# Padding the rows of the v-and-gate weights from 642 to 648 columns

## Chip, cores and metric

The kernel runs on one core of one Trainium2 chip. The metric is the device time of one execution in microseconds (us). Ratios are given with a 95% interval.

## The reference

Two branches over 2048 tokens of width 640 are mixed by a gate per token: linear attention (32 heads of 20, Hedgehog feature maps) and a SwiGLU feed-forward of width 1728.

```python
x = A_x
g = sigmoid((x * gate_w).sum(-1, keepdims=True))
a = A_ref(x, A_wqkv, A_w_phi, A_wo)      # linear attention
# inside A_ref:  kv = einsum("bhsf,bhsd->bhfd", phi_k, v);  z = phi_k summed over s
b = B_ref(x, B_w_gate, B_w_up, B_w_down) # (silu(x wg) * (x wu)) wd
return g * a + (1 - g) * b
```

## The kernel before

Tokens are cut in 16 tiles of 128. The width 640 is cut in 5 chunks of 128, which are the contraction steps. Three pieces are shown: the tile `wvg`, whose rows hold the 640 v columns of a chunk, the gate column and one spare; the ten products of a v tile, two halves of 320 and 321 columns per chunk; and the eleven products of a kv tile, whose moving operands are 63 columns each in a v buffer.

```python
wvg = sb("wvg", [P, 5, D + 2], BF16)            # P = 128, D = 640
...
v1r = sb("v1r", [P, NV, 33 * 21], BF16)         # v tiles: 33 heads of 20 values and a one
...
def v_pairs(t, pr):
    # (output, stationary, moving, start, stop, ...)
    return [(bank(2 * pr + hb, 0, 320 + hb), xT[:, t, c, :],
             wvg[:, c, 320 * hb:640 + hb - 320 * (1 - hb)],
             c == 0, c == 4, False) for c in range(5) for hb in range(2)]
...
def kvtile(t):
    b = t % 4
    pairs = []
    for j in range(NCH):                        # NCH = 11
        bk, jj = (KV0, j) if j < 8 else (KV0 + 1, j - 8)
        o = bank(bk, 63 * jj, 63 * jj + 63)
        pairs.append((o, ekr[:, b, 120 * j:120 * j + P], vbuf(t)[:, 63 * j:63 * j + 63],
                      t == 0 and jj == 0, t == NT - 1, True))
    mm(pairs)
```

The order of all work on all engines is a fixed list in the kernel. `mm` issues one matmul per entry on one line, which is why nearly all of TensorE's work carries the line L296.

The softmax here doesn't subtract the row's maximum and nothing guards it: scores larger than these inputs give would overflow.

Of the kernel before, what the change touches and what calls it, by code (L numbers as in the profile page):

```python
# [6 lines left out]
P = 128  # L7
S_TOK = 2048
D = 640
# [17 lines left out]
BF16 = DT.bfloat16  # L27
# [169 lines left out]
def _build(nc, A_x, A_wqkv, A_w_phi, A_wo, B_x, B_w_gate, B_w_up, B_w_down, gate_w, out):  # L197
# [5 lines left out]
    def sb(name, shape, dtype):  # L203
        t = nc.alloc_sbuf_tensor(name, list(shape), dtype)
        tr.reg(t, "sbuf", nc.lookup_mloc(t).addr)
        return t

    xT = sb("xT", [P, NT, 5, P], BF16)
    wqk = sb("wqk", [P, 2, 5, D], BF16)
    wvg = sb("wvg", [P, 5, D + 2], BF16)  # L210
    wog = sb("wog", [P, 5, D], BF16)
    wd = sb("wd", [P, 14, D], BF16)
    wg = sb("wg", [P, 5, F_FFN], BF16)
# [555 lines left out]
def bass_gated_mix__linear_kernel_hedgehog__swiglu_ffn__prompt_kernel(  # L769
    nc: bass.Bass,  # L770
    A_x: bass.AP,
    A_wqkv: bass.AP,
    A_w_phi: bass.AP,
    A_wo: bass.AP,
    B_x: bass.AP,
    B_w_gate: bass.AP,
    B_w_up: bass.AP,
    B_w_down: bass.AP,
    gate_w: bass.AP,
    out: bass.AP,  # L780
):
    _build(nc, A_x, A_wqkv, A_w_phi, A_wo, B_x, B_w_gate, B_w_up, B_w_down, gate_w, out)
# [28 lines left out]
```

## Time and profile before

| | before |
|---|---|
| median of the first 3 runs | 288.74 us (288.39 to 288.85) |
| span of the profiled run | 287.0 us |
| TensorE (PE) busy | 99% of the span |
| next engine (VectorE) | 57% |
| v products | 160 of 1979 matmuls |

How to read it: what a matmul costs is the distance from its start to the next one's start, called the *interval* below. In the timeline of PE the columns are start, duration of the piece, engine, line, operation, output and inputs, stationary and moving shape, and the count. A tile's cost is the start of the following piece minus its own start. Where a finer table is given, it was read start by start from the same trace, as means over the 16 token tiles; intervals of more than 160 ns are left out of the tables by chunk.

### The profile page before, as it was taken

The page shows a single profiled execution, that of the slowest core. Times are in us where ns is not written, and L with a number is a line of the kernel's source. Part 1 is how long each engine was busy: PE and PEld are TensorE (multiplying, and loading weights), DVE is VectorE, ACT ScalarE, POOL GpSimd, SP SyncE. Part 2 cuts the span into 40 slices and gives each one's busy share as a digit, 9 for nine tenths or more (in the row PEclk, how much of TensorE's full clock was granted, in tenths as well). Part 3 has the DMA queues.
Part 4 walks back from the last instruction along what each step waited for, and adds up shares of the span by engine and source line. Part 5 has one row for each costly group of instructions (what it writes and reads, how often), then busy time and mean ns, then how long its engine had stood idle before and what let it go on. Part 6 is the DMA issues. An engine that isn't in the chain of part 4 may idle for free.

```text
span 287.0 us, 4972 instructions
## 1 busy us (share of the span) xinstructions
PE 284.1 (99%) x1979; PEld 174.5 (61%) x1979; DVE 163.3 (57%) x243; ACT 152.4 (53%) x256; POOL 159.8 (56%) x125
## 2 busy tenths in 40 slices
PE   8999999999999999999999999999999999999997
PEld 6667777575644545557775556675554446666776
DVE  2337748576569978689991465970317899100000
ACT  0767778576775465683535753225676552234112
POOL 8286999879446789836543438350754558501000
PEclk9999999999999999999999999999999999999999
DMA  7977697000010598202383002061020006210101
GB/s 234 192 113 127 113 279 279 3 1 2 0 50 0 123 290 162 50 2 50 66 157 69 6 1 50 2 149 43 2 50 0 3 1 123 53 46 0 49 23 48
DMA packets 48944, 21.62 MB, mean 75 GB/s; under 512 B 39384, under 2 KB 48792, under 8 KB 48920
## 3 DMA queue, kind: packets, MB, share of 16 engines
q1 hardware_dynamic: 47400, 20.43, 31.5%
q10 hardware_dynamic: 1520, 0.87, 1.0%
q8 instruction: 16, 0.26, 0.4%
q14 instruction: 8, 0.07, 0.1%
HBM read 9.29 MB, written 2.62 MB: 42 GB/s over the span
## 4 chain that ended last, share of the span: by engine, by line
PE 99%; DVE 0%; issue 0%
PE ps L296 97%; PE ps L478 1%; PE ps L308 0%; DVE xT L320 0%; DVE osb L737 0%; DVE wvg L320 0%
## 5 line engine op out<-in xcount | busy, mean ns | idle before, releaser
L324 POOL TENSOR_TENSOR hT<-hT,us 128x512 bf16<-128x512 bf16 (+1 forms) x56 | 65.0, 1174 | 65.1 <-DVE hT L328 47.5
L328 DVE SCALAR_TENSOR_TENSOR hT<-hT,ps 128x512 bf16<-128x512 bf16 (+1 forms) x56 | 37.4, 683 | 66.8 <-ACT hT L314 53.0
L296 PE MATMUL ps<-xT,wg 128*128 128x512 bf16 x260 | 64.6, 379 | 0.0
L296 PE MATMUL ps<-xT,wu 128*128 128x512 bf16 x260 | 64.6, 379 | 0.0
L296 PE MATMUL ps<-wd,hT 128*128 128x320 bf16 (+2 forms) x462 | 63.9, 295 | 0.0
L324 POOL TENSOR_TENSOR ph<-eq,qc 128x1320 bf16<-128x1320 bf16 x16 | 42.4, 2647 | 25.6 <-DVE qc L638 20.8
L296 PEld LDWEIGHTS ps<-wd,hT 128*128 128x128 bf16 x462 | 44.5, 98 | 17.5 <-issue 0.2
L296 PE MATMUL ps<-wqk,xT 128*128 128x320 bf16 x320 | 47.7, 299 | 0.0
L314 ACT ACTIVATE hT<-ps 128x512 bf16<-128x512 f32 (+2 forms) x64 | 36.4, 569 | 16.8 <-PE ps L296 16.5
L296 PEld LDWEIGHTS ps<-xT,wu 128*128 128x128 bf16 x260 | 25.5, 98 | 30.6
L314 ACT ACTIVATE us<-ps 128x512 bf16<-128x512 f32 (+1 forms) x56 | 33.5, 598 | 18.5 <-PE ps L296 17.3
L314 ACT ACTIVATE osb<-ps,omg 128x640 bf16<-128x640 f32 (+2 forms) x17 | 12.9, 758 | 55.4 <-PE ps L296 55.4
L296 PEld LDWEIGHTS ps<-xT,wg 128*128 128x128 bf16 x260 | 25.1, 98 | 27.8 <-ACT osb L314 0.8
L324 POOL TENSOR_TENSOR ekr<-ekr,krec 128x1280 bf16<-128x1280 bf16 x16 | 37.4, 2358 | 5.8 <-DVE krec L338 5.8
L296 PEld LDWEIGHTS ps<-wqk,xT 128*128 128x128 bf16 x320 | 30.5, 98 | 13.1 <-issue 0.4
L314 ACT ACTIVATE eq<-ps 128x640 bf16<-128x640 f32 x32 | 22.4, 704 | 20.9 <-POOL ph L324 10.8
L335 DVE TENSOR_REDUCE ksum<-ekr 128x64 f32<-128x1280 bf16 x16 | 23.5, 1471 | 11.7 <-ACT ekr L314 11.7
L314 ACT ACTIVATE ekr<-ps 128x640 bf16<-128x640 f32 x32 | 22.3, 704 | 8.7 <-PE ps L296 8.2
L335 DVE TENSOR_REDUCE qz<-eq 128x64 f32<-128x1280 bf16 x16 | 23.6, 1478 | 2.6 <-ACT eq L314 2.6
L296 PE MATMUL ps<-wog,oT 128*128 128x320 bf16 (+2 forms) x165 | 24.7, 294 | 0.0
L296 PE MATMUL ps<-wvg,xT 128*128 128x320 bf16 (+1 forms) x160 | 24.1, 299 | 0.1
L335 DVE TENSOR_REDUCE qw<-ez 128x64 f32<-128x1280 bf16 x16 | 23.6, 1477 | 0.0
(73 smaller groups left out, 188.6 us busy)
## 6 DMA issues: line engine op xcount, KB each, us to landing
out_dram<-osb SPq DMA_DIRECT2D x15, 160.0 KB, 2.0
wd<-in_B_w_down_dram SPq DMA_DIRECT2D x1, 2080.0 KB, 9.2
wg<-in_B_w_gate_dram SPq DMA_DIRECT2D x1, 1040.0 KB, 10.0
wu<-in_B_w_up_dram SPq DMA_DIRECT2D x1, 1040.0 KB, 12.2
wg<-in_B_w_gate_dram SPq DMA_DIRECT2D x1, 800.0 KB, 6.1
wu<-in_B_w_up_dram SPq DMA_DIRECT2D x1, 800.0 KB, 7.7
wog<-in_A_wo_dram SPq DMA_DIRECT2D x2, 375.0 KB, 7.1
xs<-in_A_x_dram ACTq DMA_DIRECT2D x3, 160.0 KB, 4.2
```

The source lines that it names most:

```text
L296: last = pe.matmul(o, lhsT=l, rhs=r, start=st, stop=sp_, skip_group_check=sk)
L314: return run("act", lambda: act.activation(o, i, func, scale=scale), rd, [o])
L324: return run(e, lambda: eo.tensor_tensor(o, a, b, op), [a, b], [o])
L328: return run("dve", lambda: dve.scalar_tensor_tensor(out=o, in0=a, scalar=s, in1=b, op0=op0, op1=op1), rd, [o])
L335: return run("dve", lambda: dve.tensor_reduce(o, i, AX.X, ALU.add), [i], [o])
L478: last = pe.matmul(bank(2 * pr, 0, P), lhsT=c, rhs=c, start=True, stop=True)
```

## The change

The intent is that every moving operand of the v products starts on a multiple of 16 bytes. The prediction below works out the starts. A *line* is a stretch of 16 bytes that begins on a multiple of 16, a way of counting addresses.

```diff
-    wvg = sb("wvg", [P, 5, D + 2], BF16)
+    wvg = sb("wvg", [P, 5, D + 8], BF16)
```

No instruction is added, removed or moved on any engine. All tiles behind `wvg` move up by 64 bytes.

## The prediction

> **What bounds the kernel now.** I read the page's busy shares first, then the slices, the chain that ended last, the waits of PE, and last the timeline of PE where the v products stand beside the q and k products.
>
> ```profile
> PE 284.1 (99%) x1979; PEld 174.5 (61%) x1979; DVE 163.3 (57%) x243; ACT 152.4 (53%) x256; POOL 159.8 (56%) x125
> PEclk9999999999999999999999999999999999999999
> PE 99%; DVE 0%; issue 0%
> ```
>
> TensorE is busy 99% of the span and is 99% of the chain that ended last; no other engine is over 57%, and the granted clock is full in all 40 slices. "Busy" alone would not prove that the array is full, so I looked for what PE waits for. The view of waits for PE has one line, and that wait is over before 1 us:
>
> ```profile
> PE ps L478 <- PEq L796: 0.8, 1, 0.8
> ```
>
> So the kernel is a queue of matmuls, and the time is the sum of the intervals from one matmul's start to the next one's start. What a change is worth is what it takes off those intervals.
>
> The changed operand is the moving one of the v products, 160 of the 1979 matmuls. In the groups split by form, the duration of one is all but equal to that of a q or k product of the same width:
>
> ```profile
> L296 PE MATMUL ps<-wqk,xT 128*128 128x320 bf16 x320 | 47.7, 299 | 0.0
> L296 PE MATMUL ps<-wvg,xT 128*128 128x321 bf16 x80 | 22.4, 300 | 0.0
> L296 PE MATMUL ps<-wvg,xT 128*128 128x320 bf16 x80 | 22.4, 299 | 0.1
> ```
>
> These 299 and 300 ns are latencies of overlapping matmuls, not what one costs the queue. The cost is seen in the timeline of PE, as the distance from one piece's start to the next piece's start:
>
> ```profile
> 28.37 1.52 PE L296 MATMUL ps<-wqk,xT 128*128 128x320 bf16 x10
> 29.72 0.51 PE L296 MATMUL ps<-v1r,ekr 128*128 128x63 bf16 x11
> 30.07 1.54 PE L296 MATMUL ps<-wvg,xT 128*128 128x320 bf16 x10
> 31.45 1.52 PE L296 MATMUL ps<-wqk,xT 128*128 128x320 bf16 x10
> 32.81 1.54 PE L296 MATMUL ps<-wvg,xT 128*128 128x320 bf16 x10
> ```
>
> Ten q/k products take 29.72 - 28.37 = 1.35 us and 32.81 - 31.45 = 1.36 us; ten v products take 31.45 - 30.07 = 1.38 us. A v tile is some 20 ns dearer than a q or k tile, and 16 v tiles are computed. That is the whole stake: about 0.3 us in 288.7.
>
> [...]Read start by start in the trace, the q and k products follow each other at a mean of 135.8 ns[...].
>
> **The change part by part.** The program has the same instructions in the same order on all five engines; only the row pitch and addresses move. In the built program the tile starts on a multiple of 32 bytes. With 642 columns a chunk's row is 1284 bytes, so chunks c = 0 to 4 start 0, 4, 8, 12 and 0 bytes past a 16-byte line, and the second half of a chunk, 640 bytes on, has the same remainder. With 648 columns the pitch is 1296 bytes, 81 lines exactly, and all remainders are 0. So 3 chunks x 2 halves x 16 tiles = 96 of the 160 v products change; 64 were aligned already. Intervals in the trace, start to next start, mean over the 16 tiles in ns (first half of 320 columns, second of 321 with the gate column):
>
> ```
> chunk  past a line   320 col.   321 col.
>  0        0 B         136.3      136.6
>  1        4 B         139.3      139.5
>  2        8 B         137.8      139.4
>  3       12 B         138.1      139.4
>  4        0 B         135.1      136.0
> ```
>
> The sum of a tile is 1377 ns. The aligned chunks 0 and 4 average 272.0 ns a pair; chunks 1 to 3 take 278.8, 277.2 and 277.5. If these three become like the other two, a tile costs 5 x 272.0 = 1360 ns and saves 17 to 18 ns. [...]Over 16 tiles: 16 x 17.4 = 0.28 us.
>
> Where it lies: thirteen of the tiles (3 to 15) run whole between 9.8 and 67.9 us, in a stretch where PE waits for nothing, so 13 x 17.4 = 0.23 us comes off the path. The other three are computed in parts at 5 to 11 us, between arrivals of the first x tiles, which gate the transposes; I count half of their 0.05 us. That makes 0.25 us.
>
> The rest of the change costs nothing that I can find. The copy of the gate column writes five elements at another stride (171 ns, once, on DVE). The loads move the same 1280-byte rows to other offsets. All later tiles move up by 64 bytes (6432 becomes 6496 with the rounding to 32), which keeps their remainders against 16 and 32.
>
> **The rivals.** *First, the start inside a line is not the cause*, and chunks 1 to 3 are slow for another reason, say their place in the tile or a clash with reads of the stationary operand. Then nothing moves: 288.7 us. Against it: the dear chunks are just the three that start inside a line, in early tiles computed in scattered order as in late whole ones. A 32-byte line is spoken against by chunk 4, which begins 16 bytes past a 32-byte boundary and is the cheapest of all. That matters, as after the change chunks 1 and 3 begin 16 past one too.
>
> *Second, a wait takes the place of the saved time.* PE would arrive up to 0.25 us earlier at the products that need GpSimd's scaled k values, and GpSimd works at eight or nine tenths there. The tightest such point is the first: GpSimd ends its tile at 26.06 us and PE starts on it at 26.64, a slack of 0.58; later ones have 1.0 us and more. By 26.6 us only 7 tiles have been sped up, 0.12 us. ACT frees PSUM banks with less slack (down to some 0.06 us from release to weight load), but it is fed by PE and moves with it. If this wait did appear, the time would be 288.6 to 288.7.
>
> *Third, the wv loads land sooner, or later, by their new offsets.* In the first 12 us, packets of 1280 bytes take a median of 55 ns on both queues, those into the aligned x tile among them; and the starting stage waits mostly for x. Nothing, at most 0.1 us either way.
>
> *Fourth, the 64-byte shift of all other tiles* meets some conflict in SBUF. No view here shows such a thing; it is why the slower side keeps a small chance.
>
> **Range and chances.** The time is 288.74 - 0.25, rounded to 288.5 us. The three runs of before spread over 288.39 to 288.85, 0.46 us, wider than the effect[...]. So the range is 288.0 to 288.9. Two per cent are 5.8 us, twenty times what all v products could give, so within 2% gets 0.98 and each side 0.01.
>
> **What would show it.** In the changed profile a v tile in the timeline should take 1.36 us from its start to the next piece's start, not 1.38, with chunks 1 to 3 at 136 ns; PE's view of waits should stay a single early line; the q product of the first token tile and everything after it should begin about 0.25 us earlier. If chunks 1 and 3 stay at 139 and chunk 2 drops, the line is 32 bytes. If the tiles take 1.36 us and the end does not move, look for a new wait of PE before 76 us. The prediction is wrong if the other tiles' intervals (216 ns for 512 columns, 136 for 320) change, which would be the 64-byte shift at work.

## The result

The changed kernel took 288.29 us (median of 6, 287.94 to 288.48) against 288.74 us of before in the same rounds (median of 6, 288.13 to 288.97). A ratio is computed as the mean time of one kernel's fast runs over that of the other's of the same rounds, so it is not quite the ratio of these medians: 0.9987, interval 0.9974 to 0.9999. The predicted time was 288.5, the range 288.0 to 288.9, "the same" within 2%.

The busy shares on the changed kernel's page:

```profile
PE 284.2 (99%) x1979; PEld 174.8 (61%) x1979; DVE 163.4 (57%) x243; ACT 152.3 (53%) x256; POOL 159.7 (56%) x125
```

And its view of waits for PE (engine, tile and line, what it waited for, us in total, times, longest):

```profile
PE ps L478 <- PEq L796: 0.8, 1, 0.8
```

Nothing but PE is near a limit and that view shows no new wait. The next lines are the changed kernel's timeline of PE, the same q/k, kv and v pieces as in the prediction:

```profile
28.44 1.52 PE L296 MATMUL ps<-wqk,xT 128*128 128x320 bf16 x10
29.80 0.51 PE L296 MATMUL ps<-v1r,ekr 128*128 128x63 bf16 x11
30.14 1.52 PE L296 MATMUL ps<-wvg,xT 128*128 128x320 bf16 x10
31.50 1.52 PE L296 MATMUL ps<-wqk,xT 128*128 128x320 bf16 x10
32.86 1.52 PE L296 MATMUL ps<-wvg,xT 128*128 128x320 bf16 x10
```

A v tile takes 31.50 - 30.14 = 1.36 us, as a q/k tile does, where it took 1.38. The durations printed with the pieces went from 1.54 to 1.52. Mean intervals of the v products by chunk, in ns:

```
chunk   before: 1st half  2nd half    after: 1st half  2nd half
 0              136.2      136.6             136.4      136.3
 1              139.2      139.5             135.7      136.8
 2              137.8      139.4             135.9      136.6
 3              138.1      139.4             135.8      136.7
 4              135.1      136.0             135.9      136.6
```

The thirteen whole v tiles together went from 17.908 to 17.706 us: 0.202 us, 15.5 ns a tile. Apart from the wait described below, no other group of matmuls between them and the end changed by more than some 10 ns in sum.

It helps to cut the time in two at the start of the first whole v tile. Behind the cut, to the start of the last matmul, the trace of before has 275.05 us. Profiles of unaltered repeats of the changed kernel (below) have 274.86 and 274.85 us. In front of the cut the profiles range from 9.74 to 10.36 us, with no pattern that I could tie to a kernel. The changed kernel's first profile shows both: its last matmul started only 0.05 us earlier than that of before, because its first two v products took 242 and 268 ns, where 136 is usual (see experiment 5), and because of a wait of 0.10 us at 13.4 us. That wait is seen in the timelines of both kernels around 13 us. Of before:

```profile
11.46 1.49 POOL L324 TENSOR_TENSOR wbd<-wph,bmask 128x160 bf16<-128x160 bf16 x3 [4.29 <-DMA wph<-in_A_w_phi_dram]
...
13.35 0.79 PE L296 MATMUL ps<-wbd,wT 128*128 128x140 bf16 x12
```

Of the changed kernel:

```profile
11.90 1.49 POOL L324 TENSOR_TENSOR wbd<-wph,bmask 128x160 bf16<-128x160 bf16 x3 [4.75 <-DMA wph<-in_A_w_phi_dram]
...
13.48 0.79 PE L296 MATMUL ps<-wbd,wT 128*128 128x140 bf16 x12
```

GpSimd (POOL) builds a masked weight tile as soon as the load of the feature weights has landed. In before it was done at 12.95 us and PE needed it at 13.35; here the load landed 0.44 us later, it was done at 13.39, and PE, ready at 13.38, started at 13.48. The view of waits puts the wait to the weight load's "issue", so the PE line above does not show it. The wait is absent from both repeats; it came again in two of the later experiments. I count it to the luck of the first loads; no run shows more than that it comes and goes.

### The profile page after: what moved, and what is told of

The parts are those of the page before. It is cut to its first block, busy times and chain, and to the rows that moved or that the text cites. A ratio compares the mean times of both kernels' runs of the same rounds, so it can differ in the third digit from the quotient of the medians.

```text
span 286.9 us, 4972 instructions
## 1 busy us (share of the span) xinstructions
PE 284.2 (99%) x1979; PEld 174.8 (61%) x1979; DVE 163.4 (57%) x243; ACT 152.3 (53%) x256; POOL 159.7 (56%) x125
## 4 chain that ended last, share of the span: by engine, by line
PE 99%; DVE 0%; issue 0%
PE ps L296 97%; PE ps L478 1%; PE ps L308 1%; DVE osb L737 0%
## 5 line engine op out<-in xcount | busy, mean ns | idle before, releaser
L296 PEld LDWEIGHTS ps<-xT,wu 128*128 128x128 bf16 x260 | 25.5, 98 | 30.6
L314 ACT ACTIVATE us<-ps 128x512 bf16<-128x512 f32 (+1 forms) x56 | 33.5, 598 | 18.4 <-PE ps L296 17.3
```

The lines of the kernel that those rows point to most:

```text
L296: last = pe.matmul(o, lhsT=l, rhs=r, start=st, stop=sp_, skip_group_check=sk)
L314: return run("act", lambda: act.activation(o, i, func, scale=scale), rd, [o])
```

## The experiments

Every run gave correct results. Ratios are to the kernel before in the same rounds. "Behind the cut" is the time from the first whole v tile's start to the last matmul's start: 275.05 us in before.

The expectations name these ideas by letters. Theory A: a matmul whose moving operand starts inside a 16-byte line costs some 3 ns by itself. Rival B: what moved the time is the luck of the start, or there is no such cost. Rival C: the 64-byte shift of the other tiles. Rival D: the kv products are paced by something else. "History", "flat" and "place" are refinements that experiment 3 called for. Theory L, the shared line, came last and is the one that stood.

### 1. Is the time gain that of the tiles?

The changed kernel, unaltered, twice more with 5 rounds each.

> The changed kernel once more, unaltered, to narrow the interval. Theory A (a matmul whose moving operand starts inside a 16-byte line costs the queue some 3 ns more): the 96 products give back 96 x 2.7 = 0.26 us, so a ratio near 0.9991; in the profile a v tile takes 1.36 us from start to next start. Rival B (the gain in time is mostly the start of the kernel, [...]which differs from run to run): the tiles are as fast, but the ratio comes out anywhere from 0.998 to 1.000, and the start of the first whole v tile moves by 0.1 us or more against the other profiles.

> The changed kernel a third time, on the same chip and against the same runs of before as the next one. Theory A: 12.9 to 13.6 ns per v tile times 16 give 0.2 to 0.3 us, ratio 0.999 +- the interval; from the first whole v tile's start to the last matmul's start 0.20 us less than the 275.05 us of before. If the 0.45 us between the first medians were real, the ratio would be 0.9984 again.

Measured: 288.31 us against 288.26, ratio 0.9994 (0.998 to 1.0007), and 288.43 against 288.50, ratio 1.0000 (0.9986 to 1.0014). The thirteen v tiles took 17.704 and 17.706 us, and the time behind the cut was 274.86 and 274.85 us, 0.20 less than before. The differences of the means in the three comparisons are 0.39, 0.21 and 0.10 us, on average 0.23 us. So the gain is real in the trace, to a few nanoseconds each time; a comparison of times with 5 or 6 runs of the changed kernel is not fine enough to see it. Of the 0.45 us between the first medians, the traces account for 0.20.

### 2. Is it the shift of the other tiles?

The kernel before, with 64 unused bytes behind `wvg`:

```diff
+    gap = sb("gap", [P, 32], BF16)
     wog = sb("wog", [P, 5, D], BF16)
```

> The kernel before with 64 unused bytes behind the wv tile: every later tile has the addresses of the changed kernel, the wv rows keep their pitch of 1284 bytes. Theory A: same as before, ratio 1.000, v tiles at 1.38 us with chunks 1 to 3 at 138 to 139 ns. Rival C (the 64-byte shift of the other tiles made the gain): ratio near 0.9987 and v tiles at 1.36 us, or other products' intervals changed.

Measured: 288.45 us against 288.26, ratio 1.0005 (0.999 to 1.002); behind the cut 275.05 us, v tiles 17.906 us, chunks 1 to 3 at 138 to 139 ns. In its timeline of PE (a source line lower, for the line added) the v tile is 31.49 - 30.11 = 1.38 us:

```profile
30.11 1.54 PE L297 MATMUL ps<-wvg,xT 128*128 128x320 bf16 x10
31.49 1.52 PE L297 MATMUL ps<-wqk,xT 128*128 128x320 bf16 x10
```

The shift does nothing. What counts is the rows' pitch.

### 3. The same fault made on purpose in other products

The changed kernel, with rows of 642 columns for the q/k, down and output weights:

```diff
-    wqk = sb("wqk", [P, 2, 5, D], BF16)
+    wqk = sb("wqk", [P, 2, 5, D + 2], BF16)
-    wog = sb("wog", [P, 5, D], BF16)
-    wd = sb("wd", [P, 14, D], BF16)
+    wog = sb("wog", [P, 5, D + 2], BF16)
+    wd = sb("wd", [P, 14, D + 2], BF16)
     ...   # loads and copies write [.., 0:D]
```

> The changed kernel, wv rows aligned, but the rows of the q/k weights, the down weights and the output weights made 642 columns long, so that 224 + 330 + 99 = 653 matmuls of 96 to 320 columns start 4, 8 or 12 bytes into a 16-byte line. Theory A: 653 x 2.7 to 3.3 ns = 1.8 to 2.2 us slower than the changed kernel, so about 1.5 to 1.9 us slower than before, ratio 1.005 to 1.007; the q/k and down products at 138 to 140 ns in the shifted chunks and 136 in the others. Rival B: no such cost, ratio within 0.001 of the changed kernel's. A wait that hides the cost would leave the intervals at 139 ns and the time unmoved.

Measured: 289.97 us against 288.26, ratio 1.0053 (1.0038 to 1.0068). The direction is clear of noise. But behind the cut it took 276.05 us, 1.20 more than the changed kernel, not 1.8 to 2.2. By offset the q/k products had 135.6 and 139.7 ns at 4 bytes (first and second half), 138.3 and 138.3 at 8, and 138.4 and 138.9 at 12. In the timeline of PE a q/k tile takes 30.00 - 28.63 = 1.37 us:

```profile
28.63 1.54 PE L296 MATMUL ps<-wqk,xT 128*128 128x320 bf16 x10
30.00 0.51 PE L296 MATMUL ps<-v1r,ekr 128*128 128x63 bf16 x11
```

The first half at 4 bytes, which follows an aligned product, was all but free, although the first half at 4 bytes of the v products in before (chunk 1) had cost 139.2. "A start inside a line costs 3 ns" does not account for that.

### 4. Does the cost depend on what went before?

Two looks. In the first, the changed kernel's v rows and down rows all start 8 bytes into a line, and the q/k rows have a pitch of 1288 bytes:

```diff
-    wqk = sb("wqk", [P, 2, 5, D], BF16)
-    wvg = sb("wvg", [P, 5, D + 8], BF16)
+    wqk = sb("wqk", [P, 2, 5, D + 4], BF16)
+    wvg = sb("wvg", [P, 5, D + 8], BF16)[:, :, 4:D + 8]
-    wd = sb("wd", [P, 14, D], BF16)
+    wdt = sb("wd", [P, 14, D + 8], BF16)
+    wd = wdt[:, :, 4:D + 4]
     ...   # an address and a copy follow the layout
```

> The changed kernel with all v rows starting 8 bytes into a 16-byte line (pitch 1296, start moved by 4 columns), the down weights' rows likewise, and the q/k rows at a pitch of 1288 bytes, so that pairs of aligned and of shifted products alternate. It asks whether the cost is the same for each shifted matmul. History (what the first q/k experiment showed: the first shifted matmul behind an aligned one 135.5 ns, the next 139.8, the others 138.4): down products at 138.3 ns throughout, q/k pairs 135 and 139 to 140 by turns, v tiles near 1.385 us, chunks 0 and 4 as dear as the others. Flat (each shifted one costs 2 to 3 ns by itself): both of a q/k pair at 138. Place (the dear chunks of before were dear by their place in the tile): v chunks 0 and 4 stay at 136.

In the second, the wv pitch alone is 1292 bytes:

```diff
-    wvg = sb("wvg", [P, 5, D + 2], BF16)
+    wvg = sb("wvg", [P, 5, D + 6], BF16)
```

> The kernel before with a wv pitch of 646 columns, 1292 bytes: chunks 0 to 4 start 0, 12, 8, 4 and 0 bytes past a 16-byte line, the order of before turned round. Theory A, with the size of the offset of no matter: v tiles at 1.38 us as before, chunks 1 to 3 at 138 to 140, 0 and 4 at 135 to 137. If the size of the offset mattered, the first two shifted products (139.3 and 139.5 before, at 4 bytes) would drop to 138.1 and 139.4, and the last two rise.

Measured (single executions, 288.82 and 288.53 us), v intervals in ns:

```
chunk   all 8 bytes in: 1st   2nd      pitch 1292 (0,12,8,4,0): 1st   2nd
 0              135.9        139.7                  136.2        136.2
 1              135.1        139.1                  139.3        139.5
 2              135.1        139.4                  135.2        139.4
 3              135.0        139.1                  135.0        139.7
 4              135.0        139.3                  135.1        135.8
```

In the first kernel every product starts inside a line, and only the second halves are dear. Its down products alternate too: 135.0 for the first half, 138.7 for the second; the expectation of 138.3 throughout, the "history" idea, failed. The q/k pairs came out as expected, 135 and 139 to 140. "Place" failed as well, since chunks 0 and 4 became dear. So none of the three stood.

Line numbers do account for these tables. Write down the 16-byte line in which a product's moving operand begins and the one in which its predecessor's ended. With the start moved by 8 bytes and a pitch of 1296, a first half ends in the middle of a line and the second half begins in that same line: dear (139.1 to 139.7 ns). The second half ends at byte 1290 (line 80), the next chunk begins at 1304 (line 81): free (135.0 to 135.1 ns). With pitch 1292, chunk 1 begins at 1292 in line 80, where the gate column before it ended (before byte 1282, line 80): dear. Chunk 2 begins at 2584 (line 161), and its predecessor ended at 2574 (line 160): free, although it starts inside a line. In before, with pitch 1284, chunks 1, 2 and 3 begin in the line in which the gate column before them ended, and their halves share a line too. Those are six products of ten, just the six that start inside a line. That is why before could not tell the two rules apart. In experiment 3 there is no gate column: chunk 0 ends at byte 1280, chunk 1 begins at 1284 in a new line, and is free (135.6 ns). The table of pitch 1292 speaks for 16 bytes as the size too: chunks 1 and 2 both begin 10 bytes past their predecessor's end, the first across a multiple of 8 and none of 16 (139.3 ns), the second across a multiple of 16 and none of 32 (135.2 ns).

### 5. The two rules set against each other

One kernel removes the sharing and leaves every start where it was; the other keeps every start aligned and makes the halves share a line.

The kernel before, with two orders turned round:

```diff
-                 c == 0, c == 4, False) for c in range(5) for hb in range(2)]
+                 c == 0, c == 4, False) for c in range(5) for hb in (1, 0)]
...
-        for j in range(NCH):
+        for j in range(NCH - 1, -1, -1):
...
-                          t == 0 and jj == 0, t == NT - 1, True))
+                          t == 0 and j in (7, NCH - 1), t == NT - 1, True))
```

> The kernel before, rows of 642 columns and all addresses as before, but with the two halves of a v chunk taken in the other order (second half first) and the eleven kv products from the last to the first. No operand's start moves; but no matmul now begins in the 16-byte line in which its predecessor's moving operand ended. Theory L (shared line: the cost falls on a matmul whose moving operand begins in the line where the one before it ended; it fits the second halves at 139 and the first halves at 135 of the run with all v rows 8 bytes into a line): v tiles at 1.36 us, kv tiles at 0.32 us or less, from the first whole v tile to the last matmul 0.65 us less than before (274.40 us), ratio near 0.998. Theory A (a start inside a line costs by itself): v tiles stay at 1.38 us and kv tiles at 0.345, ratio 1.000.

The changed kernel, first halves four columns wider:

```diff
-        return [(bank(2 * pr + hb, 0, 320 + hb), xT[:, t, c, :], wvg[:, c, 320 * hb:640 + hb - 320 * (1 - hb)],
+        return [(bank(2 * pr + hb, 0, (324, 321)[hb]), xT[:, t, c, :], wvg[:, c, 320 * hb:(324, 641)[hb]],
```

> The changed kernel, all rows aligned, but the first half of each v product takes 324 columns instead of 320 (its last four results are not used; the output stays right). Every operand starts on a 16-byte line, but the second half begins in the line in which the first one ended. Theory L: second halves at 139 to 141 ns. Theory A: second halves stay at 136.7. [...]

Measured: with the orders turned, the v tiles took 17.719 us, within 0.015 us of the padded kernel's 17.705, with no operand's address touched. With aligned but overlapping halves the second halves took 139.1 to 140.1 ns, the first ones 136.6 to 137.6. The timeline of PE with the orders turned (the repeat of experiment 6):

```profile
29.86 0.49 PE L296 MATMUL ps<-v1r,ekr 128*128 128x63 bf16 x11
30.18 1.53 PE L296 MATMUL ps<-wvg,xT 128*128 128x321 bf16 x10
31.55 1.52 PE L296 MATMUL ps<-wqk,xT 128*128 128x320 bf16 x10
```

And with aligned starts and a shared line:

```profile
30.38 1.54 PE L296 MATMUL ps<-wvg,xT 128*128 128x324 bf16 x10
31.76 1.52 PE L296 MATMUL ps<-wqk,xT 128*128 128x320 bf16 x10
```

The first has misaligned starts and a v tile of 31.55 - 30.18 = 1.37 us (1.363 on average); the second has aligned starts and 1.38 (1.382 on average, of which some 8 ns are the four added columns, by an estimate: in before 512 columns take 216 ns and 320 take 135.8, which makes 0.42 ns a column, and twenty columns are added in a tile). The shared line is the cause of what the padding removed, and the alignment of the start is not, in itself. It is not the only thing that costs a few ns. With the orders turned, the second halves of chunks 2 and 3 still took 139.0 and 137.4 ns (138.9 and 136.9 in the repeat), and the 22 kv products that start 6 bytes into a line 33.1 ns, where those at the other offsets took 28.6 to 30.6. None of them begins in the line in which its predecessor ended. For this rest I have no reason.

The time of the turned kernel was 288.40 us against 288.50, ratio 1.0007 (0.9983 to 1.0031), and one of its six executions took 290.47 us. The profiled execution lost its gain in front of the cut. Its timeline of PE, where the first v products start:

```profile
5.05 1.64 PE L296 MATMUL ps<-wvg,xT 128*128 128x321 bf16 x6
6.53 0.44 PE L308 MATMUL ps<-ident,xs 128*128 128x128 bf16 x5
```

Six products took 1.64 us, where a changed kernel's profile (the second repeat) has 0.99:

```profile
5.08 0.99 PE L296 MATMUL ps<-wvg,xT 128*128 128x320 bf16 x6
5.91 0.44 PE L308 MATMUL ps<-ident,xs 128*128 128x128 bf16 x5
```

Four of the six intervals were 267 ns, about twice the usual 136, and a fifth 246. The granted clock is 1.00 for this run, and it reads 1.00 from 0 to 7 us in the changed kernel's first profile, which has two such intervals. So five v products were slow at the start of this profile, two at that of the changed kernel's first one (242 and 268 ns), none at that of before (147 ns at most, but for one interval of 167 that ends in a wait). Why, no trace or run here shows.

### 6. A version that beats both

The kv products were the place to look. In before they take 28.4 ns where they begin on a 16-byte line and 31.4 to 32.8 elsewhere. They lie end to end in the v buffer, 126 bytes each, so 140 of the 176 begin in the line where their predecessor ended. Two ways to avoid that were tried: 64 columns for each three heads, on top of the padded wv rows,

```diff
-    v1r = sb("v1r", [P, NV, 33 * 21], BF16)
+    v1r = sb("v1r", [P, NV, 12 * 64], BF16)
...
-   wvg[:, c, 320 * hb:640 + hb - 320 * (1 - hb)]     # halves of 320 and 321
+   wvg[:, c, 360 * hb:(360, 641)[hb]]                # 360 and 281: 18 heads, then 14 and the gate
...
-   vbuf(t)[:, 63 * j:63 * j + 63]
+   vbuf(t)[:, 64 * j:64 * j + 63]
    ...   # ones, the PSUM copy and the warm-up products follow the layout
```

or only the order of the kv products turned round, from the last to the first (the second and third hunk of experiment 5's diff on the changed kernel).

> Both the changed kernel and the same idea for the kv products: in the profile of before these 63-column matmuls take 28.4 ns where they start on 16 bytes and 31.4 to 32.9 elsewhere. The v buffers get 64 columns per three heads, so that all 176 start on 16 bytes; the v halves become 360 and 281 columns (same sum), and ACT's copy of a v tile grows from 640 to 720 elements. Theory A with a cost per matmul whatever its width: about 155 x 3.3 = 0.5 us less than the changed kernel, ratio to before near 0.997, an 11-matmul kv tile at 0.31 us from start to next start in place of 0.35. Rival D: the kv products are paced by their weight loads or by ACT's longer copy, and the time stays at the changed kernel's, ratio 0.9985 to 0.999.

> The version with aligned kv products again, to compare it with the changed kernel over the same rounds of before. The first run gave 0.9982. Theory A: 0.35 us less in the changed kernel's stretch from first whole v tile to last matmul (274.51 against 274.86 us), so about 0.0012 below the ratio of the changed kernel in these rounds. Rival D: no difference.

> The kernel before with both orders turned round, again: [...]one of its six executions stood out at 290.47 us. Theory L: from the first whole v tile to the last matmul 274.59 us again, 0.46 less than before, and, where the start is as in before (first whole v tile at 9.7 to 9.9 us), a time near 288.1 and a ratio of 0.998 to 0.999. Rival (the new order makes the start slower): the first whole v tile starts at 10.3 us or later again and the ratio stays at 1.000 or above.

> The changed kernel with only the kv products turned round (from the last to the first). Theory L: v tiles 1.36 us from the padding, kv tiles 0.327 us from the order as in the run with both orders turned; 0.50 us less than before from the first whole v tile to the last matmul, 274.55 us; ratio to before 0.998. Theory A: kv tiles at 0.345 us, 274.85 us, ratio 0.999.

| kernel | median, before | ratio (95%) | behind the cut | kv tile |
|---|---|---|---|---|
| before | | | 275.05 us | 346 ns |
| changed, first repeat | 288.31, 288.26 | 0.9994 (0.998 to 1.0007) | 274.86 | 345 |
| changed + 64 columns | 287.85, 288.26 | 0.9982 (0.9969 to 0.9996) | 274.51 | 320 |
| the same again | 287.63, 288.50 | 0.9974 (0.996 to 0.9988) | 274.50 | 320 |
| before, both orders turned, again | 288.07, 288.75 | 0.9986 (0.9963 to 1.0009) | 274.59 | 327 |
| changed + kv order turned | 288.26, 288.75 | 0.9981 (0.9967 to 0.9995) | 274.72 | 327 |

The 64-column version is 0.35 us faster than the changed kernel behind the cut, in two profiles, and its interval against before is below 1 both times. Its timeline of PE has a kv tile at 29.93 - 29.61 = 0.32 us, where before had 30.07 - 29.72 = 0.35:

```profile
29.61 0.48 PE L296 MATMUL ps<-v1r,ekr 128*128 128x63 bf16 x11
29.93 1.52 PE L296 MATMUL ps<-wvg,xT 128*128 128x360 bf16 x10
```

ACT's copy of a v tile grew from about 0.71 to 0.78 us and no cost of it is seen: in its first profile ACT still stood idle before these copies until PE was done, 3.5 us in all. Turning the kv order alone, on the changed kernel, gives most of that without touching the kv layout, 327 ns; the rest of 7 ns a tile lies mainly in the products that start 6 bytes into a line (33.5 ns each in that run, 28.1 to 30.6 at the other offsets). Both expectations had been larger: 0.5 us less than the changed kernel for the 64 columns, where 0.35 came, and 274.40 us for the turned orders, where 274.59 came. The turned kv order's 274.72 us holds the early wait for the masked weights again, 0.14 us (an interval of 351 in place of 216 ns). Without it, it would be 274.58. The slow start of the kernel with both orders turned did not repeat in full: its first whole v tile came at 10.04 us, against 10.36 in its first profile and 9.81 in before. One of its six executions again took much longer (289.85 us), as one had the first time; no other kernel had such runs, and what they are stays open.

### What a shared line costs

Worked out from intervals, over the count of matmuls that begin in their predecessor's last line:

| where | extra time | shared lines | each |
|---|---|---|---|
| v products of before (13 tiles) | 17.908 - 17.705 = 0.203 us | 78 | 2.6 ns |
| kv products of before, against the 64-column version | 5.531 - 5.121 = 0.410 us | 140 | 2.9 ns |
| q/k, down, output products of experiment 3 | 1.23 us | 491 | 2.5 ns |
| q/k, v, down products of the first of experiment 4 | 0.170 + 0.127 + 0.438 us | 80 + 65 + 210 | 2.1 ns |

These are net figures: a second half that shares a line takes 139 to 140 ns, some 3 to 4 more than 135.8, but the next product without a shared line takes 135.0 to 135.3 and gives part of that back. The width of the product makes little difference: 63 columns pay 2.9 ns, 320 and 321 pay 2.6.

## Why the prediction was right, and where its reason was not

- **The bound and the size.** Right. PE's intervals were the whole story. Predicted were 17.4 ns a tile and 0.23 us on the thirteen whole tiles; the trace gave 15.5 ns and 0.20 us. The difference lies in chunk 4: the aligned mean was taken partly from it, the cheapest in before (135.1 and 136.0), which fits its place behind dear products; in the changed kernel it went up to 135.9 and 136.6.
- **The time.** Predicted 288.5, measured 288.29 in a range of 288.0 to 288.9. The measured difference of the first medians, 0.45 us, was larger than the 0.25 predicted, and two repeats gave 0.10 and 0.21 us in the means. The prediction's statement that the spread of the runs exceeds the effect was right.
- **The cause: the step that failed.** The prediction held that a product whose moving operand starts inside a 16-byte line costs more by itself, and dismissed its first rival, that "the start inside a line is not the cause". Experiment 5 shows that the rival was right in its first half: the cost falls on a product that begins in the line in which its predecessor ended. In before the two rules name the same six products of a tile, so the table of intervals, read as evidence for one, was evidence for both. The change worked because rows of 81 whole lines, halves of 40 whole lines and a gate column at the end leave no shared line. That the right size came with a wrong reason is luck: the padding to 648 columns ended both conditions at once. The dear v products of before (137.8 to 139.5 ns) begin in the line just read; those that begin in a new one took 135.1 to 136.6.
- **The second rival**, a new wait, was looked for at the scaled k values (26 us, slack 0.58 us); nothing waited there. The early wait that did appear in one profile, at 13.4 us, had a slack of 0.4 us in before, less than the one called the tightest. It was the late landing of a load in that execution and not PE's lead that used it up.
- **The third rival** stays untested: the part in front of the cut varies by 0.6 us, more than any such effect.
- **The fourth rival**, the 64-byte shift: excluded by experiment 2.
- **What would show it.** The v tile at 1.36 us and chunks 1 to 3 near 136 ns came as written. That everything behind would begin 0.25 us earlier did not hold in the one profile taken (0.05 us), for the slow first products and the early wait; behind the cut it held in the repeats, with 0.20 us.

## What to carry to other kernels

When TensorE is the bound, look at the intervals between matmul starts, chunk by chunk, and not at durations: a pattern of 3 ns shows there and not in the mean duration of one matmul, which rose here from 299 and 300 to 301 and 302 ns. Lay out or order the matmuls so that none begins in the 16-byte line in which the one before it ended, which cost 2.1 to 2.9 ns each here; padding the rows does it (17.908 to 17.706 us for the thirteen v tiles), and so does taking neighbouring pieces in the reverse order (17.719 us), which costs no memory and gave most of it here (274.59 us behind the cut, where the best version had 274.50). And when two rules pick out the same instructions, build one kernel that separates them before believing either.
